# The last eight chunks of linear attention as pairs of 64 tokens, one step a slot

## The chip, the cores and the metric

The kernel runs on one core of one Trainium2 chip. The core has a matrix engine (TensorE, here PE, with its weight loads as PEld), a vector engine (DVE), a scalar engine (ACT) and a queue that issues DMAs (SP). The metric is the device time of one launch in microseconds (us); lower is better.

## The reference

```python
# linear attention with decay, 4 sequences x 8 heads x 768 tokens x 64
for t in range(S):
    state = gamma * state + einsum('bhd,bhe->bhde', k[:, :, t], v[:, :, t])
    y[:, :, t] = scale * einsum('bhd,bhde->bhe', q[:, :, t], state)
x = y as 3072 tokens x 512 features
# first MLP
h = x @ w_in                          # 512 -> 2048
x = (h * sigmoid(1.702 * h)) @ w_out  # 2048 -> 512
# second MLP, its own weights
h = x @ moe2_w_in
g = maximum(h, 0) + alpha * minimum(h, 0)
out = g @ moe2_w_out
```

All is float32; the kernel splits the operands of the MLPs into a high and a low part and multiplies those, and it runs attention in float32 itself.

## The kernel before

The 3072 tokens are 24 chunks of 128 (`C`), six to a sequence, and four chunks make a block of 512 columns (`BT`) for the MLPs. A state of 64x64 for each head is carried from chunk to chunk and starts anew every sixth chunk.

Attention runs beside the MLPs. A table `jobs` gives each piece of work a slot, and the MLP loops call `run(slot)` as they go. In the first part (slots up to 63, `base` = 64) a step of the first MLP on blocks 0 and 1 is 24 products of 512 columns and covers two slots. From then on (the loop over `units`, L1069) the MLPs run as seven products on a 2x2 grid of blocks; a unit is six products (`h_unit`, L763), and a slot comes after the fourth and after the seventh unit of each seven. Chunks 0 to 7 are done in the lead-in and the first part, chunks 8 to 15 in the first part from slot 36 on, and chunks 16 to 23 (the last eight) in slots `base` to `base` + 8, between the first units.

A chunk has two forms. In the **whole** form `att_scores` scales v on ACT (eight operations, L337), makes the scores of 128 tokens into two banks of PSUM (L344), and DVE multiplies both by the causal mask (L355). A slot later `att_out` (L372) makes the state update, the output from the chunk and the output from the state; `att_state` keeps the state in `diag` (L409, L412), and `att_x_kept` writes the outputs (L442). In the **half** form a chunk is two halves of 64 tokens, so that every product is 64x64 and uses a quarter of the array. `half_step(o, new)` issues in one step the outputs of the chunk before (`o`) and the scores and state updates of the next one (`new`), turn by turn (L481). DVE then masks the scores in one operation (L543), makes `mid`, the state between the halves (L557, or a copy on ACT at the start of a sequence, L555), the next state `hstate` (L561, L562), and the outputs (L572). `half_v_scale` (L471) scales v in a slot of its own, ahead of the step.

Before, chunks 8 to 15 are half and two slots apart, and all others whole. The two forms keep the state in another layout: `swap_state` moves it between them with three small DMAs on SP, once ahead of chunk 8 and once behind chunk 15.

q, k and v of the last eight come by `load_early(c)`, four DMAs of 256 KB on SP, in slots `LOADS` + `base`. Every engine takes its instructions in the order that the program's scheduler gave them, and `tc.high_priority` moves some ahead. That order is fixed when the program is built.

Of the kernel before, what the change touches and what calls it, by code (L numbers as in the profile page):

```python
# [19 lines left out]
P = 128  # L20
C = 128
# [54 lines left out]
def tile_linear_attention_two_mlps(ctx: ExitStack, tc, qk, kv, w1, w2, consts, alpha, out):  # L76
# [246 lines left out]
    att, xl = {}, {}  # L323

    def att_psum(c, which, shape):
        early = EARLY[c] if c < BT // C else EARLY[1] if c >= 4 * BT // C else {}
        if which in early:
            tag = early[which]
            return (ps_h if tag == "h" else ps_y).tile(shape, F32, tag=tag, name=which)
        return ps_a.tile(shape, F32, tag="a", name=which)  # L330
# [81 lines left out]
            nc.vector.tensor_tensor(out=diag, in0=src, in1=dec, op=ALU.mult)  # L412

    def att_x(c):
        if c >= 2 * BT // C:
            att_x_kept(c)
            return
        x32 = take("x32", (P, NP, C))
        early_x = c == BT // C - 1
        banks = att[c][0] if early_x else att[c]  # L420
        for n in range(2):
            px = banks[n][:, :2 * C].rearrange("p (n i) -> p n i", n=2)
            with tc.high_priority(HG):
                nc.vector.tensor_tensor(out=x32[:, n::2, :], in0=px, in1=decay_out[:, n::2, :], op=ALU.mult)
        j, i = divmod(c, BT // C)
        cols = slice(i * C, (i + 1) * C)
        if i == 0:
            new_x(j)
        nc.scalar.copy(out=x_hi[j][:, :, cols], in_=x32)  # L429
        if early_x:  # L430
            att_state(c)
        att[c] = x32

    def att_x_kept(c):
        banks = att.pop(c)
        t, i = divmod(c % (2 * BT // C), BT // C)
        for k in range(2):
            for d in range(2):
                if i == 0:
                    xl[k, d, t] = take("xl")  # L440
                with tc.high_priority(HG):
                    nc.vector.tensor_tensor(  # L442
                        out=xl[k, d, t][:, i * C:(i + 1) * C], in0=banks[k][:, d * C:(d + 1) * C],
                        in1=decay_out[:, 2 * d + k, :], op=ALU.mult,
                    )

    def att_x_low(c):
        j, i = divmod(c, BT // C)
# [12 lines left out]
        for s in range(2):  # L461
            nc.sync.dma_start(out=out[ROWS[s], 0::2, :], in_=src[ROWS[1 - s], 0::2, :])

    def half_psum(which):
        return (ps_h if which == "sc" else ps_a).tile([P, 512], F32, tag="h" if which == "sc" else "a", name=which)

    def half_v_scale(c):
# [59 lines left out]

    def half_step(o, new):
        if o is not None:
            att["px", o] = half_psum("px")  # L530
        if new is not None:
            att["sc", new] = half_psum("sc")
            att["pu", new] = half_psum("pu")
        half_products(o, new)
        if o is not None:
            give(att.pop(("v", o)), att.pop(("a", o)), att.pop(("mid", o)))
            leave("qk", o)
        if new is not None:
            leave("kv", new)
        with tc.high_priority(HG):  # L540
            if new is not None:
                a = att["a", new] = take("a", (P, 2 * NP, HC))
                nc.vector.tensor_tensor(  # L543
                    out=a, in0=att.pop(("sc", new)).rearrange("p (n i) -> p n i", i=HC),
                    in1=half_causal.unsqueeze(1).to_broadcast([P, 2 * NP, HC]), op=ALU.mult,
                )
                half_state(new)
            if o is not None:
                half_x(o)
# [13 lines left out]

    def half_x(c):
        px = att.pop(("px", c)).rearrange("p (n i) -> p n i", n=NP)
        n = c - 2 * BT // C
        t, i = divmod(n, BT // C)
        for k in range(2):
            for d in range(2):
                if i == 0:  # L570
# [332 lines left out]
    def job(slot, fn, *args, load=()):  # L903
        jobs.setdefault(int(slot), []).append((fn, args, load))

    def attention(c, s_scores, s_out, s_x, s_low):
        if c < 4 * per:
            job(s_scores, att_scores, c, load=(("qk", c), ("kv", c)))
        else:
            job(LOADS[c - 4 * per] + base, load_early, c)  # L910
            job(s_scores, att_scores, c)
        job(s_out, att_out, c)
        job(s_x, att_x, c)
        if c < 2 * per:
            job(s_low, att_x_low, c)

    def convert(key, slot):
        job(slot, conv_words, key, load=(key,))
# [8 lines left out]

    turn_at = {}
    for c in range(NCH):
        if 2 * per <= c < 4 * per:  # L930
            s = ATT1 + 2 * (c - 2 * per)
            turn_at.setdefault(s, {})["new"] = c
            turn_at.setdefault(s + 2, {})["o"] = c
            if c in RINGED:
                job(s - 1, half_v_scale, c, load=(("qk", c), ("kv", c)))
            else:
                job(s - 4, load_early, c)
                job(s - 1, half_v_scale, c)
            continue
        if c < per:  # L940
            s = 2 * c - 2 * per - 1
        elif c < 2 * per:
            s = 2 * (c - per)
        else:
            s = base + c - 4 * per
        attention(c, s, s + 1, s + 1, s + 2)
    for s, t in turn_at.items():
        job(s, half_step, t.get("o"), t.get("new"))
    job(2 * per + 4, swap_state, hstate[2 * per % 2], diag)
    job(ATT1 + 4 * per, swap_state, diag, hstate[4 * per % 2])  # L950
    for ft in range(NF):
        for n, kind in enumerate(("in", "out")):
            m = 2 * ft + n
# [218 lines left out]
```

## Time and profile before

| | |
|---|---|
| median of three timed runs | 1036.85 us (1035.78 to 1038.05) |
| profiled execution, span of its instructions | 1037.7 us |
| PE busy | 1019.7 us, 98% |
| DVE busy | 873.8 us, 84% |
| ACT busy | 679.3 us, 65% |
| DMA | 289.8 MB, 279 GB/s over the span |

The profiled execution is one run of its own; the page gives its span and nothing around it, and the span lies 0.85 us above the median. A busy PE is not PE at its peak: a product of 512 columns shows about 389 ns, but the next starts about 0.23 us after it, since they are pipelined. So what a stretch costs on PE is read from starts, not from busy time.

### The profile page before, as it was taken

The page shows a single profiled execution, that of the slowest core. Times are in us where ns is not written, and L with a number is a line of the kernel's source. Part 1 is how long each engine was busy: PE and PEld are TensorE (multiplying, and loading weights), DVE is VectorE, ACT ScalarE, POOL GpSimd, SP SyncE. Part 2 cuts the span into 40 slices and gives each one's busy share as a digit, 9 for nine tenths or more (in the row PEclk, how much of TensorE's full clock was granted, in tenths as well). Part 3 has the DMA queues.
Part 4 walks back from the last instruction along what each step waited for, and adds up shares of the span by engine and source line. Part 5 has one row for each costly group of instructions (what it writes and reads, how often), then busy time and mean ns, then how long its engine had stood idle before and what let it go on. Part 6 is the DMA issues. An engine that isn't in the chain of part 4 may idle for free.

```text
span 1037.7 us, 18658 instructions
## 1 busy us (share of the span) xinstructions
PE 1019.7 (98%) x6316; PEld 837.9 (81%) x6316; DVE 873.8 (84%) x1738; ACT 679.3 (65%) x1405; POOL 0.2 (0%) x4
## 2 busy tenths in 40 slices
PE   7999999898999999999999999999999999999998
PEld 5778888787888888888888888888888888888886
DVE  6999845997989999888899999998677978677792
ACT  6887835466776885765886776775555855556740
POOL 0000000000000000000000000000000000000000
PEclk9999999998999999999999999999999999999999
DMA  8689939689999889989989899896786766775671
GB/s 326 228 266 396 349 118 368 228 320 319 385 392 388 268 310 370 324 309 357 341 286 361 276 320 334 294 314 180 228 274 212 220 215 194 226 245 178 187 203 61
DMA packets 147231, 289.80 MB, mean 279 GB/s; under 512 B 17472, under 2 KB 17856, under 8 KB 147136
## 3 DMA queue, kind: packets, MB, share of 16 engines
q1 hardware_dynamic: 146848, 288.30, 80.8%
q8 instruction: 50, 0.82, 0.3%
q10 hardware_dynamic: 288, 0.31, 0.1%
q14 instruction: 45, 0.37, 0.1%
HBM read 213.83 MB, written 74.45 MB: 278 GB/s over the span
## 4 chain that ended last, share of the span: by engine, by line
PE 85%; DVE 8%; DMA 4%; ACT 1%; SPq 1%; issue 0%; DVEq 0%; ACTq 0%
PE py L836 37%; PE pa L763 21%; PE pd L763 16%; PE py L680 5%; PE ph L661 4%; DMA wcin<-wb 2%; DVE wb L229 1%; PE px L372 1%; DVE s L271 1%; PE sc L344 1%; DMA early<-kv 1%; DVE gl L645 1%; DMA ld<-kv 1%; DVE a L355 1%; DMA early<-qk 1%; DVE cvt L210 0%
## 5 line engine op out<-in xcount | busy, mean ns | idle before, releaser
L836 PE MATMUL py<-gh,yw 128*128 128x512 f32 x1120 | 299.5, 389 | 0.0
L836 PEld LDWEIGHTS py<-gh,yw 128*128 128x128 f32 x1120 | 210.2, 188 | 43.7
L763 PE MATMUL pa<-xo,hw 128*128 128x512 f32 x912 | 231.0, 390 | 0.0
L763 PEld LDWEIGHTS pa<-xo,hw 128*128 128x128 f32 x912 | 170.9, 188 | 35.8
L645 DVE TENSOR_TENSOR gl<-gw,gh 128x512 fp32r<-128x512 f32 x240 | 161.1, 687 | 42.9 <-ACT gh L644 36.9
L644 ACT CAST gh<-gw 128x512 fp32r<-128x512 f32 x240 | 145.7, 620 | 53.6 <-PE py L836 24.3
L763 PE MATMUL pd<-xo,hw 128*128 128x512 f32 x684 | 173.3, 389 | 0.0
L836 PE MATMUL py<-gl,yw 128*128 128x512 f32 x560 | 172.6, 389 | 0.0
L763 PEld LDWEIGHTS pd<-xo,hw 128*128 128x128 f32 x684 | 128.2, 188 | 26.8
L836 PEld LDWEIGHTS py<-gl,yw 128*128 128x128 f32 x560 | 105.1, 188 | 21.8
L850 DVE TENSOR_TENSOR yc<-py,yc 128x512 f32<-128x512 f32 x99 | 63.7, 684 | 26.2 <-PE py L836 26.2
L637 DVE SCALAR_TENSOR_TENSOR gw<-t,nalpha,gw 128x512 f32<-128x512 f32 x96 | 71.4, 748 | 15.5 <-ACT gw L636 15.3
L635 ACT ACTIVATE t<-gw 128x512 f32<-128x512 f32 x72 | 45.5, 632 | 52.7 <-DVE gw L778 49.8
L225 ACT CAST wb<-s 128x256 fp32r<-128x256 f32 x128 | 48.3, 402 | 41.4 <-DVE s L271 27.6
L680 PE MATMUL py<-gh,wb 128*128 128x512 f32 x256 | 67.3, 405 | 3.2 <-ACT gh L644 2.8
L661 PE MATMUL ph<-xhi,wb 128*128 128x512 f32 x256 | 64.2, 392 | 1.2 <-ACT xhi L429 1.2
L775 ACT COPY gw<-pa 128x512 f32<-128x512 f32 x80 | 46.8, 585 | 26.3 <-PE pa L763 25.7
L680 PEld LDWEIGHTS py<-gh,wb 128*128 128x128 f32 x256 | 47.9, 192 | 15.4 <-ACT gh L644 4.1
L661 PEld LDWEIGHTS ph<-xhi,wb 128*128 128x128 f32 x256 | 47.6, 188 | 11.6 <-ACT xhi L429 1.3
L778 DVE TENSOR_TENSOR gw<-pd,gw 128x512 f32<-128x512 f32 x80 | 54.8, 685 | 2.2 <-PE pd L763 2.1
L229 DVE TENSOR_TENSOR wb<-s,wb 128x256 fp32r<-128x256 f32 x128 | 50.0, 419 | 7.1 <-ACT wb L225 6.9
L799 DVE TENSOR_TENSOR gw<-gw 128x512 f32<-128x512 f32 x80 | 53.9, 688 | 0.3
(119 smaller groups left out, 1358.4 us busy)
## 6 DMA issues: line engine op xcount, KB each, us to landing
hw<-wcin SPq DMA_DIRECT2D x266, 256.0 KB, 4.7
yw<-wcout SPq DMA_DIRECT2D x232, 256.0 KB, 3.8
ld<-w SPq DMA_DIRECT2D x64, 512.0 KB, 5.9
wcin<-wb SPq DMA_DIRECT2D x112, 256.0 KB, 5.1
wcout<-wb SPq DMA_DIRECT2D x88, 256.0 KB, 4.2
yw<-wo SPq DMA_DIRECT2D x48, 256.0 KB, 5.1
wo<-wb SPq DMA_DIRECT2D x32, 256.0 KB, 6.3
early<-qk SPq DMA_DIRECT2D x26, 256.0 KB, 6.0
```

Of the source, the lines that this page charges most:

```text
L225: nc.scalar.copy(out=w[:, 0:256], in_=src)
L229: nc.vector.tensor_tensor(out=w[:, 256:], in0=src, in1=w[:, 0:256].bitcast(F32), op=ALU.subtract)
L637: nc.vector.scalar_tensor_tensor(out=g, in0=t, scalar=nalpha[:, ft:ft + 1], in1=g, op0=ALU.mult, op1=ALU.add)
L644: nc.scalar.copy(out=gh, in_=g)
L645: nc.vector.tensor_tensor(out=gl, in0=g, in1=gh.bitcast(F32), op=ALU.subtract)
L661: nc.tensor.matmul(out=ph, lhsT=cols(w, low, k), rhs=x[:, k, :], start=(n == 0), stop=(n == len(prods) - 1),)
L680: nc.tensor.matmul(out=py[e], lhsT=lhsT, rhs=g, start=(begin and seen[e] == 1), stop=(end and seen[e] == 3))
L763: nc.tensor.matmul(out=ps, lhsT=w[:, 256 * part_ + k * P:256 * part_ + (k + 1) * P], rhs=x[2 * k + low], start=(n in (0, 1, 3) and m == 0) ...
L778: nc.vector.tensor_tensor(out=g, in0=ps, in1=g, op=ALU.add)
L799: sub = lambda o, x, y: nc.vector.tensor_tensor(out=o, in0=x, in1=y, op=ALU.subtract)
L836: nc.tensor.matmul(out=ps[e], lhsT=w[:, at:at + P], rhs=t, start=(fresh and seen[e] == 1), stop=(m == GQ - 1 and seen[e] == 3), skip_group ...
L850: add_ = lambda o, x: nc.vector.tensor_tensor(out=o, in0=ps, in1=x, op=ALU.add)
```

## The change

Chunks 16 to 23 take the half form as well. Their steps come every slot (not every second one as for chunks 8 to 15), v is scaled one slot ahead of its step, and the loads keep their slots. Scores go to banks `y0` and `y3` in turn, state updates to `y1`, outputs to `y2`. The state stays in the half layout, so the second `swap_state` goes. The host lays out the arrays for all chunks from 8 on in halves.

```diff
     def att_x(c):
-        if c >= 2 * BT // C:
-            att_x_kept(c)
-            return
...
-    def half_psum(which):
+    def half_psum(which, c):
+        if c >= 4 * BT // C:
+            tag = {"sc": f"y{3 * (c % 2)}", "pu": "y1", "px": "y2"}[which]
+            return ps_y.tile([P, 512], F32, tag=tag, name=which)
         return (ps_h if which == "sc" else ps_a).tile([P, 512], F32, tag="h" if which == "sc" else "a", name=which)
...
     for c in range(NCH):
-        if 2 * per <= c < 4 * per:
-            s = ATT1 + 2 * (c - 2 * per)
+        if c >= 2 * per:
+            late = c - 4 * per
+            s, after = (base + late, 1) if late >= 0 else (ATT1 + 2 * (c - 2 * per), 2)
             turn_at.setdefault(s, {})["new"] = c
-            turn_at.setdefault(s + 2, {})["o"] = c
+            turn_at.setdefault(s + after, {})["o"] = c
             if c in RINGED:
                 job(s - 1, half_v_scale, c, load=(("qk", c), ("kv", c)))
             else:
-                job(s - 4, load_early, c)
+                job(LOADS[late] + base if late >= 0 else s - 4, load_early, c)
                 job(s - 1, half_v_scale, c)
             continue
-        if c < per:
-            s = 2 * c - 2 * per - 1
-        elif c < 2 * per:
-            s = 2 * (c - per)
-        else:
-            s = base + c - 4 * per
+        s = 2 * c - 2 * per - 1 if c < per else 2 * (c - per)
         attention(c, s, s + 1, s + 1, s + 2)
...
-    job(ATT1 + 4 * per, swap_state, diag, hstate[4 * per % 2])
```

What the change moves on the engines. On PE, the end of the first of the nine steps and the start of the second, with the units between (`sc` are scores, `pu` state updates and `px` outputs, each a bank of PSUM; `a` masked scores, `v` scaled v); before:

```order
L344 MATMUL sc_3503<-early 128x128
L763 MATMUL pa<-xo,wb 128x512 x12
L763 MATMUL pd<-xo,wb 128x512 x6
L372 MATMUL px<-v,early 64x64 x8
L372 MATMUL px<-a_3512,v 64x64
```

and now:

```order
L468 MATMUL sc<-early 64x64 x16
L468 MATMUL pu<-v,early 64x64 x16
L749 MATMUL pa<-xo,wb 128x512 x12
L749 MATMUL pd<-xo,wb 128x512 x6
L468 MATMUL px<-early,hstate_82 64x64
```

The steps stand at the same places between the units. The first step, which held eight rows of scores, now also holds the updates of the state, which stood in the second step before. Over all nine steps there were 296 rows and are 488; a row of a float32 product is two instructions in the trace. Elsewhere PE's order is the same.

On ACT, the end of the first part of the program, with the last two pairs of `g` and `gh`, the activations that the products `py` of the first MLP wait for (`v` is the scaled v, `wb` and `xo` are pieces of weights and of x); before:

```order
L632 ACTIVATE g_3270<-ph_3257 128x512
L644 CAST gh_3272<-g_3270 128x512
L225 CAST wb_3413<-s12_3356 128x256
L225 CAST wb_3421<-s34_3357 128x256
L225 CAST wb_3415<-s12_3356 128x256
L225 CAST wb_3423<-s34_3357 128x256
L588 CAST xo_3300<-xl_2577 128x512
L588 CAST xo_3300<-xl_2581 128x512
L632 ACTIVATE g_3338<-ph_3325 128x512
L588 CAST xo_3371<-t2_3121 128x512
L644 CAST gh_3340<-g_3338 128x512
```

and now:

```order
L458 ACTIVATE v_3539<-early_3320,cst_78 128x64 x5
L618 ACTIVATE g_3267<-ph_3254 128x512
L458 ACTIVATE v_3539<-early_3320,cst_78 128x64
L630 CAST gh_3269<-g_3267 128x512
L458 ACTIVATE v_3539<-early_3320,cst_78 128x64
L225 CAST wb_3419<-s12_3353 128x256
L225 CAST wb_3427<-s34_3354 128x256
L225 CAST wb_3421<-s12_3353 128x256
L574 CAST xo_3297<-xl_2577 128x512
L574 CAST xo_3297<-xl_2581 128x512
L618 ACTIVATE g_3335<-ph_3322 128x512
```

The scaling of v for chunk 17 (`v_3539`; one more of its eight stands just ahead of these rows) now comes ahead of the last two pairs of `g` and `gh`, and that of chunk 16 around the pair before those; both stood behind the last pair. Of the four casts of `wb` between the pairs three are left there, and the fourth comes behind the last `gh`.

On SP, the loads of chunk 17 (`early`, two for q and k and two for k and v), before:

```order
L249 DMA wcin1_6_96<-wb_3284 128x512
L249 DMA wcin1_6_96<-wb_3286 128x512
L286 DMA wo_3293<-wo0_122 128x512
L178 DMA early_3317<-qk 128x512
L178 DMA early_3319<-qk 128x512
L178 DMA early_3321<-kv 128x512
L178 DMA early_3323<-kv 128x512
```

and now:

```order
L178 DMA early_3218<-kv 128x512
L286 DMA wo_3294<-wo1_123 128x512
L178 DMA early_3314<-qk 128x512
L178 DMA early_3316<-qk 128x512
L178 DMA early_3318<-kv 128x512
L178 DMA early_3320<-kv 128x512
L249 DMA wcout1_7_113<-wb_3226 128x512
```

They stood behind the stores to `wcout1_7` and `wcin1_6` and now stand ahead of both.

## Rows read from the trace of the kernel before

**Rows 1.** The page, first part: busy time, share of the span, instructions.

```profile
PE 1019.7 (98%) x6316; PEld 837.9 (81%) x6316; DVE 873.8 (84%) x1738; ACT 679.3 (65%) x1405; POOL 0.2 (0%) x4
```

**Rows 2.** Windows: stretch, length, busy time by engine, clock, DMA share, GB/s.

```profile
246.00:320.00 74.00, 74.00 (x807) 60.61 (x806) 62.21 (x158) 49.33 (x124) 0.00 (x0) 0.99 1.01 373
```

**Rows 3.** Timeline of PE, whole steps: start, length, line, operation, tiles, shapes, count.

```profile
252.87 1.16 PE L344 MATMUL sc<-early 64*128 64x128 f32 x16
253.96 0.50 PE L763 MATMUL pa<-xo,wb 128*128 128x512 f32 x1
...
266.94 0.27 PE L372 MATMUL px<-a,v 128*64 128x64 f32 x1
...
269.47 1.66 PE L763 MATMUL pd<-xo,wb 128*128 128x512 f32 x6
...
282.01 0.69 PE L372 MATMUL px<-v,early 128*64 128x64 f32 x16
...
285.01 3.02 PE L763 MATMUL pa<-xo,hw 128*128 128x512 f32 x12
...
313.96 0.27 PE L372 MATMUL px<-a,v 128*64 128x64 f32 x1
315.40 0.73 PE L763 MATMUL pa<-xo,hw 128*128 128x512 f32 x2
```

**Rows 4.** Timeline of PE, half steps of chunks 8 to 15.

```profile
139.93 1.15 PE L481 MATMUL sc<-ld 64*64 64x64 f32 x32
...
141.94 2.11 PE L680 MATMUL py<-gh,wb 128*128 128x512 f32 x8
...
147.61 0.27 PE L481 MATMUL px<-ld,hstate 64*64 64x64 f32 x1
...
149.63 2.11 PE L680 MATMUL py<-gh,wb 128*128 128x512 f32 x8
...
206.52 0.68 PE L481 MATMUL px<-early,hstate 64*64 64x64 f32 x16
208.53 0.50 PE L680 MATMUL py<-gh,wb 128*128 128x512 f32 x1
```

**Rows 5.** Timeline of PE around 241 us; in brackets idle time and its releaser.

```profile
235.93 1.98 PE L680 MATMUL py<-gh,wb 128*128 128x512 f32 x8
...
241.65 3.78 PE L680 MATMUL py<-gh,wb 128*128 128x512 f32 x8 [2.84 <-ACT gh L644]
```

**Rows 6.** Windows, the stretch at the lower clock.

```profile
240.84:247.67 6.83, 6.02 (x14) 4.78 (x15) 5.56 (x12) 6.06 (x22) 0.00 (x0) 0.50 0.67 252
```

**Rows 7.** The chain of waits from 225 to 262 us: start, length, engine, tile, line.

```profile
236.83 1.09 DVE s L271 x3
...
238.63 0.03 ACT wb L225
...
241.07 0.53 ACT gh L644
```

**Rows 8.** Timeline of ACT.

```profile
233.61 0.62 ACT L644 CAST gh<-g 128x512 fp32r<-128x512 f32 x1
...
242.02 3.93 ACT L337 ACTIVATE v<-early,cst 128x64 f32<-128x64 f32 x16
```

**Rows 9.** Timeline of SP, DMA issues.

```profile
225.03 2.25 SPq L249 DMA_DIRECT2D wcout<-wb  x4
...
233.17 0.92 SPq L178 DMA_DIRECT2D early<-kv  x2
...
265.86 1.73 SPq L178 DMA_DIRECT2D early<-kv  x2
```

**Rows 10.** Tile `early` from 215 to 290 us.

```profile
DMA to landing us min/median/max: 3.8/5.3/6.3
```

**Rows 11.** Timeline of PE, a half step that waited.

```profile
196.64 0.29 PE L481 MATMUL px<-early,hstate 64*64 64x64 f32 x2 [1.66 <-DVE hstate L561]
...
200.86 0.50 PE L680 MATMUL py<-gh,wb 128*128 128x512 f32 x1
```

More of the change, by code (lines that the diff above doesn't have):

```diff
@@ L325, in att_psum @@
     def att_psum(c, which, shape):
-        early = EARLY[c] if c < BT // C else EARLY[1] if c >= 4 * BT // C else {}
+        early = EARLY[c] if c < BT // C else {}
         if which in early:
@@ L432, in att_x @@
         att[c] = x32
[L434 to L445, printed above, removed]
     def att_x_low(c):
@@ L529, in half_step @@
         if o is not None:
-            att["px", o] = half_psum("px")
+            att["px", o] = half_psum("px", o)
         if new is not None:
-            att["sc", new] = half_psum("sc")
-            att["pu", new] = half_psum("pu")
+            att["sc", new] = half_psum("sc", new)
+            att["pu", new] = half_psum("pu", new)
         half_products(o, new)
@@ L565, in half_x @@
         px = att.pop(("px", c)).rearrange("p (n i) -> p n i", n=NP)
-        n = c - 2 * BT // C
-        t, i = divmod(n, BT // C)
+        t, i = divmod(c % (2 * BT // C), BT // C)
         for k in range(2):
@@ L906, in attention @@
     def attention(c, s_scores, s_out, s_x, s_low):
-        if c < 4 * per:
-            job(s_scores, att_scores, c, load=(("qk", c), ("kv", c)))
-        else:
-            job(LOADS[c - 4 * per] + base, load_early, c)
-            job(s_scores, att_scores, c)
+        job(s_scores, att_scores, c, load=(("qk", c), ("kv", c)))
         job(s_out, att_out, c)
         job(s_x, att_x, c)
-        if c < 2 * per:
-            job(s_low, att_x_low, c)
+        job(s_low, att_x_low, c)
     def convert(key, slot):
@@ L936, in tile_linear_attention_two_mlps @@
             else:
-                job(s - 4, load_early, c)
+                job(LOADS[late] + base if late >= 0 else s - 4, load_early, c)
                 job(s - 1, half_v_scale, c)
             continue
-        if c < per:
-            s = 2 * c - 2 * per - 1
-        elif c < 2 * per:
-            s = 2 * (c - per)
-        else:
-            s = base + c - 4 * per
+        s = 2 * c - 2 * per - 1 if c < per else 2 * (c - per)
         attention(c, s, s + 1, s + 1, s + 2)
@@ L1140, in chosen @@
         n = np.arange(NCH)[:, None, None]
-        return np.where((n >= 2 * BT // C) & (n < 4 * BT // C), half, whole)
+        return np.where(n >= 2 * BT // C, half, whole)
     def weights(w_in, w_out, swap):
```

## The prediction

> **What bounds the kernel now.** I read the page first. PE is busy for 98% of the span, far ahead of DVE and ACT [rows 1]; since a busy PE need not be at its peak, that alone says only that PE seldom stands still. Next I cut out the stretch in which the last eight chunks run. From 246 to 320 us PE is busy for all of its 74.00 us, at a granted clock of 0.99 [rows 2]. So no wait is to be had there; time can only come from fewer or shorter products, and a stall of another engine costs something only if it becomes a wait of PE. The same row shows the DMA engines full (share 1.01, 373 GB/s). Third I read, from starts, what attention takes of PE there. Last I looked at the only long hole of PE near this stretch: it waits 2.84 us for `gh` ahead of 241.65 [rows 5], and from 240.84 to 247.67 the granted clock is 0.50, the lower of the two levels (1.2 of 2.4 GHz) [rows 6].
>
> **The steps on PE, before.** A step's price is the time from its first product to the next product of the units. The first (scores of chunk 16 alone) takes 253.96 - 252.87 = 1.09 us; a step at the edge of a sequence (outputs without state, or without an update) 269.47 - 266.94 = 2.53, and there are two; a full one 285.01 - 282.01 = 3.00, and there are five; the last (outputs alone) 315.40 - 313.96 = 1.44 [rows 3]. Sum: 1.09 + 2 x 2.53 + 5 x 3.00 + 1.44 = 22.59 us.
>
> **The steps after.** The trace of before has this very step, for chunks 8 to 15. With new work alone it takes 141.94 - 139.93 = 2.01 us for 64 instructions; with both parts 149.63 - 147.61 = 2.02 for 128; with old work alone 208.53 - 206.52 = 2.01 [rows 4]. The step with both takes no longer than one with half as much, because scores and outputs use different quarters of the array; that is where the gain is. Nine steps: 2.01 + 7 x 2.02 + 2.01 = 18.16 us. PE gains 22.59 - 18.16 = 4.43 us. The first step is dearer by 0.92 and the last by 0.57; the seven between give 5.9. The bounds: the steps could not well be under 2.0, so 4.6 at most; if products did not overlap, at the pace of the step with new work alone (2.01 / 64 = 31 ns), 976 instructions would take 30.6 us, a loss of 8.0. I take 4.43, because the same instructions in the same order were timed here.
>
> The Trainium skill speaks against the change on this point: "TensorE: Matmul & The Clock Gate", section "Wait — 56ns, not 53.3ns?", says that matmuls never start closer than about 25 ns, however few columns they have. By that, 976 instructions would take an estimated 24.4 us, and the change would lose 1.8. Here the trace disagrees: 2.02 us for 128 is 16 ns each [rows 4].
>
> **DVE and ACT.** For a chunk DVE does two masks, two state operations and four outputs before, and one mask, three state operations and the same four outputs after: one operation of 512 columns less, one of 256 more. ACT does one copy more for each sequence. PE never waits for either in this stretch [rows 2], so I count nothing for it. What counts is when they come, and three things move.
>
> First, the hole at 241.65. The chain of waits leads to it through DVE's sums (ending at 236.83 + 1.09 = 237.92), the last of four `wb` casts on ACT (238.63), and `gh` (ending 241.60) [rows 7]. In the new order that last cast stands behind `gh`. The third can start when the sums end, at about 238.0, so ACT gets to x and `g` some 0.6 us sooner, and PE starts at about 241.0. As PE then runs at half speed until 247.67 [rows 6], half of that is lost again: gain 0.3 us. Against it stands the scaling of v for chunks 16 and 17, now ahead of the last two pairs. Sixteen scalings took 3.93 us [rows 8], 0.25 each. Seven of chunk 17 come ahead of the next-to-last `gh`, which ended at 233.61 + 0.62 = 234.23 while PE wanted it at 235.93 [rows 5, 8]: 1.7 us more against a slack of 1.7, so a wait of 0.0 to 0.2. Those of chunk 16 stand around the pair before; ACT, idle for a third of the span [rows 1], should have room for them. Bounds for this place: 0.7 gained to 0.8 lost without a change of the clock; I take 0.2 gained.
>
> Second, the scaling now waits for a load. v of chunk 20 is scaled about a slot sooner than before, and its load is issued from 265.86 to 267.59 [rows 9] and lands about 5.3 us later [rows 10], so at up to 273. Behind half of that scaling stands the copy of `mid` for chunk 18 on ACT, behind that DVE's outputs of chunk 17, and for their bank the step of PE that I expect at about 273 (a slot of 7 to 8 us behind the one at 266.94 [rows 3], less 0.9 gained by then). If the load lands as late as before, this step waits 1 to 1.5 us. But four stores that stood ahead of the loads of chunk 19 go out earlier, while SP has little to do, so I expect the loads behind them some 2 to 3 us earlier. The copies of `pa` behind the scalings of chunks 21 and 22 have a slack of the same size. Bounds 0 to 2.5 us; I take 0.4 lost, near the lower end, because the order of the DMAs speaks for it.
>
> Third, the loads of the units' weights. PE reaches them up to 4.5 us sooner and DMA is full [rows 2]. The earlier stores help here too. I count nothing; at worst a wait of 1 us near 310.
>
> The three DMAs of the second swap go; nothing on PE waited for them.
>
> **Sum.** -4.43 - 0.2 + 0.4 = -4.2 us. Against the profiled execution that is a span of 1037.7 - 4.2 = 1033.5. The median of the runs lies 0.85 under that span, so the forecast is 1036.85 - 4.2 = 1032.6 us, 0.4% faster.
>
> **Rivals.**
>
> *The state comes late.* In chunks 8 to 15 one step waited for `hstate` on DVE, 1.66 us ahead of it, and then took 200.86 - 196.64 = 4.22 in place of 2.02 [rows 11]: 3.9 us in one step. DVE takes its work in a fixed order, and in the new one two of the state chains stand behind sums that wait for DMAs or behind the late copy of `mid`. Against it: the chain has a slot of some 8 us ((313.96 - 282.01) / 4 [rows 3]) and needs about 2 us of DVE, and the whole form, with the same slots and a chain of the same kind, made PE wait nowhere [rows 2]. One such wait gives 1032.6 + 3.9 = 1036.5, no change; a smaller one of 2 us gives 1034.6. Chance 0.17.
>
> *The clock stays up.* The hole at 241.65 gets shorter. If the clock does not fall there, PE is spared (247.67 - 241.65) / 2 = 3.0 us [rows 5, 6], and the time is 1029.6. For it: the fall came late in the hole, at 240.84, 0.8 us ahead of its end. Against it: the hole keeps more than 2 us. Chance 0.10.
>
> *The load of chunk 17 lands late (slower).* Seven scalings of it now stand on ACT ahead of a `gh` that PE wants at 235.93 [rows 5]. Before, that load was issued up to 234.1 [rows 9] and so landed at about 239 (5.3 us later, [rows 10]). If it still lands then, `gh` follows at about 242 (seven scalings 1.7, `g` and `gh` 1.2) and PE stands for 6 us; all that follows, the last hole too, moves by about 5.5, and the clock falls sooner or once more for up to 3.4 us. The sum is then between 1032.6 + 5.5 = 1038.1 and 1041.5; I put 1040. It decides from a landing at 237.8 on; up to 233 nothing is lost. Against it: the load now stands ahead of the stores that SP issued from 225.03 [rows 9], so it should land near 230. Chance 0.06.
>
> *The small products do not overlap*, in other banks than before, so that the change doesn't do what it says: 1032.6 + 4.4 + 8.0 = 1045 at the pace of 31 ns, or 1032.6 + 4.4 + 1.8 = 1038.8 by the 25 ns above. Against it: seven steps of the same form. Chance 0.03.
>
> **How the numbers follow.** The forecast has 0.64, and its own range is 1031 to 1034.4. What this kernel's measurement can tell from no change is about 0.2%, 2.1 us, so faster means under 1034.8. Faster: 0.64, and 0.10 for the clock, and about 0.03 of the late state with a small wait: 0.77. Same: the rest of the late state, 0.14, and 0.01 of the others. Slower: 0.08. The range for 8 in 10 goes from 1029.3, with the clock up, to 1035.3, with a wait of some 2.7 us.
>
> **What will show it.** Nine steps on PE of 2.0 us each, at the places of the old ones; PE busy throughout from about 246 to 316; the first `y` product behind the hole at about 241.0, and the clock at 0.50 behind it. The step after the start of the sequence at chunk 18 shows whether `mid` came late: any idle time of PE named for DVE or ACT there is the second item. The forecast is wrong if a step takes over 2.3 us, if PE waits anywhere from 246 to 316 for more than 1 us in sum, or if a hole appears at 236.

## The result, and the profile after

The change made the kernel slower. Its median is 1042.66 us over 6 runs (1040.14 to 1044.45), against 1036.48 us (1035.20 to 1038.05) of the kernel before in the same rounds; the ratio is 1.0054 [1.0041, 1.0067]. The forecast was 1032.6 us, with a range from 1029.3 to 1035.3.

The profiled executions show 3.6 us of this: the span is 1041.3 us, where it was 1037.7. In the kernel after and in every later run the span is 1.7 to 2.1 us shorter than the time of the same execution; by that, an estimate, the span of 1037.7 belongs to some 1039.5 us, more than any of the six runs of before here took, and so the spans show less of the loss than the medians. The page of the kernel after has these lines on the engines and on one DMA queue:

```profile
PE 1017.2 (98%) x6700; PEld 835.2 (80%) x6700; DVE 871.9 (84%) x1738; ACT 676.2 (65%) x1406; POOL 0.2 (0%) x4
...
q8 instruction: 54, 0.88, 0.3%
```

The first answers to [rows 1]. PE has 384 products more, and is busy for 2.5 us less, in a span that is longer: it stands still more. The last line is a queue that the prediction did not look at. It carries instructions, in packets of 16 KB, and will decide this case.

The stretch of [rows 2] is no longer full. By windows (busy time of PE, PEld, DVE, ACT, POOL, then granted clock, DMA share, GB/s):

```profile
243.00:317.00 74.00, 67.67 (x1161) 55.59 (x1161) 58.38 (x151) 44.99 (x114) 0.00 (x0) 0.95 0.97 356
...
283.53:286.95 3.42, 3.15 (x8) 2.50 (x9) 3.28 (x10) 2.50 (x10) 0.00 (x0) 0.50 1.02 382
293.77:297.19 3.42, 3.42 (x9) 2.71 (x9) 1.88 (x7) 0.56 (x1) 0.00 (x0) 0.50 1.04 385
```

PE is idle for 6.3 of 74 us, and the granted clock is at its lower level twice, for 3.42 us each, where it was there once, from 240.84 to 247.67 [rows 6]. PE's own rows, from its timeline (in brackets idle time and its releaser), show where it stands:

```profile
240.53 0.73 PE L666 MATMUL py<-gh,wb 128*128 128x512 f32 x2 [2.00 <-ACT gh L630]
243.39 0.84 PE L749 MATMUL pa<-xo,wb 128*128 128x512 f32 x3
...
272.04 0.50 PE L749 MATMUL pa<-xo,hw 128*128 128x512 f32 x1 [0.36 <-ACT gw L618]
...
278.69 0.21 PE L468 MATMUL px<-early,hstate 64*64 64x64 f32 x1 [0.91 <-DVE s L271]
...
283.80 0.76 PE L749 MATMUL pa<-xo,hw 128*128 128x512 f32 x1 [3.02 <-ACT gw L618]
...
293.20 0.21 PE L468 MATMUL pu<-v,early 64*64 64x64 f32 x1 [1.80 <-issue]
...
317.40 0.97 PE L749 MATMUL pa<-xo,hw 128*128 128x512 f32 x3
```

The first row answers to [rows 5]: that hole went from 2.84 to 2.00 us and the clock did not fall in it, so the units start at 243.39, 3.55 us ahead of before. What follows gives more than that back. The nine half steps, from their first product to the next product of the units, as [rows 3] were read:

```
start   248.92 255.24 262.93 269.26 278.69 289.57 300.99 307.69 315.38
length    2.01   2.02   2.02   2.78   5.12   4.13   2.38   2.04   2.01   sum 24.5 (forecast 18.16)
```

Five are what was forecast. The fourth, fifth, sixth and seventh are not, and 0.91 us of waiting stands ahead of the fifth. From the first unit to the product behind the last step PE took 315.40 - 246.94 = 68.46 us before and takes 74.01 now, 5.55 more; the start 3.55 sooner leaves 2.0 us lost on PE. The other 1.6 us of the profile lie behind PE's last product (5.92 us to the end of the span, 4.32 before), in the landing of the last outputs; later runs show 4.3 there for kernels like before and anything from 4.2 to 6.3 for kernels like after, so I leave it out.

### The profile page after: what moved, and what is told of

Same layout as the page of the kernel before. It is cut to its first block, busy times and chain, and to the rows that moved or that the text cites. A ratio compares the mean times of both kernels' runs of the same rounds, so it can differ in the third digit from the quotient of the medians.

```text
span 1041.3 us, 19427 instructions
## 1 busy us (share of the span) xinstructions
PE 1017.2 (98%) x6700; PEld 835.2 (80%) x6700; DVE 871.9 (84%) x1738; ACT 676.2 (65%) x1406; POOL 0.2 (0%) x4
## 4 chain that ended last, share of the span: by engine, by line
PE 77%; DVE 10%; DMA 7%; ACT 4%; issue 1%; SPq 0%; DVEq 0%; ACTq 0%
PE py L822 37%; PE pa L749 20%; PE pd L749 15%; DMA ld<-kv 3%; PE ph L647 2%; DVE wb L229 2%; PE py L666 2%; DMA early<-kv 1%; DVE s L271 1%; DMA ld<-w 1%; DMA wcin<-wb 1%; DVE gl L631 1%; PE px L468 1%; ACT v L458 1%; DVE cvt L210 1%
```

## The experiments

Four theories stood at one time or another. A: ACT stands for late loads at the head of its queue (it does wait: four times, 8.1 us in all), and what is queued behind it holds PE. B: PE runs out of instructions. C, later D: DVE is late for the next step; as D, it frees the one PSUM bank of `px` too late. F: what PE gains is given back to engines that are full.

Two numbers are counted in each trace. PE's instructions (weight loads, products, semaphore instructions) are numbered by their start, from 0: 13,766 after, 12,993 before. Divided by 256 that is 53.8 and 50.8, and the queue q8 carries 54 packets of 16 KB after and 50 before, so one packet is 256 instructions of 64 bytes. The page of before:

```profile
q8 instruction: 50, 0.82, 0.3%
```

And the holes at 283.80 and 293.20 stand at the numbers 6081 and 6337, the wait at 278.69 at 5825: each leaves 193 when divided by 256. Such a number is called a border. The fifth half step (5825 to 6080) is exactly one packet. Count the packets along with the borders, the first packet for 449, the next for 705, and so on: PE passes none of the 1043 borders of the 20 traces sooner than 2.18 us behind the start of its packet.

Each trace is one execution, and executions of one program differ. PE's 2000th product of the program's own, which comes ahead of the place of every edit but e3's, starts between 191.67 us (e13) and 196.01 (e6); e14 and e18 are the same program, and are 2.7 us apart at the 2200th (206.10 and 208.79). So times are compared by medians and intervals, and the traces are read for where PE stands.

**First four: theory A against theory B.** e1 moves the loads, e2 the scaling of v, e3 the packets' borders, e4 does to the kernel before what A blames.

```diff
-LOADS = (-5, -3, -1, 1, 2, 3, 4, 5)                                       # e1
+LOADS = (-6, -4, -2, -1, 0, 1, 2, 3)
-                job(s - 1, half_v_scale, c)                               # e2, chunks 16 to 23, ranked ahead of half_step
+                job(s, half_v_now, c)
+    for _ in range(64):                                                   # e3, behind the warm products
+        nc.tensor.matmul(out=idle[:, :32], lhsT=warm[:, :P], rhs=warm[:, :32], start=True, stop=True)
+            job(s_scores - 1, whole_v_scale, c)                           # e4, in the kernel before
```

> The changed kernel with the loads of the last eight chunks one to two slots earlier (slots -6, -4, -2, -1, 0, 1, 2, 3 from the start of the late part, where they were -5, -3, -1, 1, 2, 3, 4, 5); nothing else differs. Theory A (ACT: the scaling of v now stands one slot nearer to its load, waits for it at the head of ACT's queue, and the gates and copies behind it hold PE): the wait of 2.91 us ahead of 276.64 and the PE hole of 3.02 us ahead of 283.80 go, and with the hole one of the two stretches at the lower clock (3.41 us, half of it lost, 1.7): 1042.7 - 4.7 = 1038. Theory B (PE runs out of instructions inside dense half steps): the hole of 1.80 us inside a half step stays or moves to another one; by B alone the time stays within 1 us of 1042.7. Theory C (DVE's chain of state and products of x is late): no hole of PE ahead of a half step goes, 1042 to 1043.

> The changed kernel with v of chunks 16 to 23 scaled in the slot of its half step, ahead of it, and not one slot before; loads as in the changed kernel. Theory A: ACT's waits for loads (8.1 us in four waits) shrink to under 1 us, since each load has some 7 us more; but the update products of the same half step now wait for eight scalings of 0.25 us, so up to 2 us of PE in each of eight steps: between 1038 (the scalings find ACT free) and 1050. Theory B: the hole of 1.8 us inside one half step stays, whatever ACT does; alone 1042.7. Theory C: no change, 1042 to 1043.

> The changed kernel with 64 more products of 32 columns on PE at the very start, beside the warm products, where PE waits for the first loads: 128 instructions, half of one 16 KB packet of instructions (64 bytes each, by 0.88 MB in 54 packets and one packet per 256 instructions). Theory B: where the packets begin within the late half steps moves by half a packet, so the hole of 1.80 us inside the half step at 289.57 goes and one like it comes in another half step, or none: 1039 to 1043. Theory A and theory C: the hole at 293.20 has nothing to do with packets and stays where it is; 1042.7.

> The kernel before, its last eight chunks in their whole form, with one difference: v of chunks 16 to 23 is scaled one slot earlier, as in the changed kernel, with the loads where they were. Theory A: ACT stands for the loads as in the changed kernel, and gates and copies behind it hold PE: one hole of about 3 us and one stretch at the lower clock of 1.7 us lost, 1036.5 + 3 to 5 = 1039.5 to 1041.5. Theory B and theory C: nothing that they speak of is changed, 1036.5 within 1 us.

Measured: e1 1044.63 us, ratio to before 1.0073 [1.0056, 1.0090]; e2 1040.47, 1.0033 [1.0019, 1.0047]; e3 1040.73, 1.0041 [1.0026, 1.0057]; e4 1037.51, 1.0004 [0.9993, 1.0015].

As the cause of the two large holes theory A falls with e1. ACT waits for no load there any more, and both are there, at the same instruction numbers 6081 and 6337. PE's timeline of e1, and ACT's gate that the first row names:

```profile
285.52 0.63 ACT L618 ACTIVATE gw<-gw 128x512 f32<-128x512 f32 x1 [0.34 <-DVE gw L764]
```

```profile
286.70 4.46 PE L749 MATMUL pa<-xo,hw 128*128 128x512 f32 x12 [2.90 <-ACT gw L618]
...
297.08 0.27 PE L468 MATMUL px<-early,mid 64*64 64x64 f32 x1 [2.74 <-issue]
```

The gate had ended 0.55 us before PE went on, so it did not hold PE; a releaser is inferred, and here it is only the last thing that happened. In the kernel after it ended at 283.79, by chance just ahead of 283.80. e2 shows the same hole without such a chance:

```profile
277.77 0.21 PE L471 MATMUL px<-early,hstate 64*64 64x64 f32 x1 [0.20 <-DVE s L271]
...
283.43 4.56 PE L752 MATMUL pa<-xo,hw 128*128 128x512 f32 x12 [3.57 <-issue]
```

e3 moves the borders by half a packet, and all nine half steps take 2.01 to 2.02 us; one wait of 1.95 us for `px` is left, ahead of a step. Its time is little better, though: 1.0041, with an interval that overlaps that of the kernel after (1.0041 to 1.0067). Its trace is 3.7 us behind the one of the kernel after at PE's 2000th product, and its own products take 1.75 us there; what made the rest is not shown, and e6, whose edit comes later, is 2.9 behind at the same product. e4 says little on A, as its ACT waits for a load only 0.40 us.

**Next four: moving the borders in an idle place.** The same small products stand where PE waits for `gh` at 240.

```diff
+    fill = ps_a.tile([P, 512], F32, tag="a", name="fill")
+    some = cst.bitcast(BF16)
+    for _ in range(54):                                                   # e5, e7, e8; 80 in e6
+        nc.tensor.matmul(out=fill[:, :32], lhsT=some[:, :P], rhs=some[:, :32], start=True, stop=True)
     for s, step in queue:
         finish_step(s, step)
```

> The changed kernel with 54 small products of 32 columns (108 PE instructions) put where PE waits for gh before the last step ahead of the units, 2.00 us there; at the 27 ns apiece that 64 like them took at the start of e3 (1.75 us) they need 1.5 us, inside that wait. Theory B (instructions): PE's instructions come in packets of 256, and all three late holes (0.91, 3.02, 1.80 us) stand at instruction numbers that leave 193 when divided by 256, since from 5825 to 6081 a whole packet is one half step, used up in 2.0 us. 108 instructions more move the borders so that no packet is used up in under 5.4 us by the steps' own times: the three holes (5.7 us) go, and with them the two stretches at the lower clock (3.41 us each, half of it lost, 3.4 together): 1042.7 - 9.1 = 1033.6. Theory A (ACT waits for loads): nothing of it is changed, the waits of ACT for loads (8 us) stay, and the hole of 3.02 us charged to the gate stays: 1042.7 or at best 1041 for the clock ahead.

> As e5, but 80 products (160 instructions, 2.2 us of work in the same wait). Theory B: the borders now lie so that the seventh half step, the one that starts at 300.99 in the changed kernel, is a whole packet of its own (2.0 us): the holes at the fourth to sixth half step go, and one of 2 to 3 us comes at the end of the seventh, with a stretch at the lower clock (1.7 us): 1033.6 + 0.2 + 4 = 1038, and some 4 us slower than e5. Theory A: 54 and 80 products make no difference, and no hole comes at the seventh half step.

> The kernel before with the same 54 products in the same place, its late chunks whole. By theory B no packet there is used up in under 9 us in that part, so moving the borders does nothing; what is left is what filling the wait does to the clock: 3.41 to 6.83 us at the lower clock in the kernel before, of which half is lost: 1036.9 - 0 to 3.4 = 1033.5 to 1036.9. If e5 gains far more than this one, the filler's effect on e5 is that of the borders.

> e5 and the earlier loads of e1 together, so that neither ACT's waits nor the packets should be left. Theory B: within 1 us of e5. Theory A, in so far as ACT's waits for loads cost time beside the packets: 1 to 3 us under e5. Earlier loads that hurt by themselves (e1 measured 1044.6): 1 to 3 us above e5.

Measured: e5 1038.87 us, 1.0019 [1.0004, 1.0033]; e6 1044.65, 1.0065 [1.0048, 1.0082]; e7 1037.54, 1.0000 [0.9986, 1.0014]; e8 1042.24, 1.0044 [1.0031, 1.0057].

80 products against 54 make 5.8 us; at 27 ns apiece the 26 more explain 0.7 of it. How much of the rest is the place of a border is not shown: the stretch of the half steps is 71.15 us in the trace of e6 and 69.61 in that of e5, and e6 is 3.5 us behind already at the 2000th product, ahead of the edit. The hole came where theory B had it, at the seventh half step and behind (PE, e6), now at the numbers 6849 and 7105:

```profile
301.69 1.55 PE L749 MATMUL pd<-xo,hw 128*128 128x512 f32 x6 [1.11 <-ACT cvt L192]
...
310.75 0.33 PE L468 MATMUL px<-early,mid 64*64 64x64 f32 x4 [2.87 <-issue]
```

But e5 kept only 3.8 of the 9.1 us that B promised. With the border holes gone, other waits stand in their place (PE, e5): `px` held by DVE, and far behind, a gate with a stretch of 3.41 us at the lower clock. This trace is of the longest of e5's 11 executions, 3.4 us above their median, so not all of it need stand in the others.

```profile
286.72 0.24 PE L468 MATMUL px<-early,hstate 64*64 64x64 f32 x1 [1.91 <-DVE xl L558]
...
412.74 1.65 PE L749 MATMUL pa<-xo,hw 128*128 128x512 f32 x6 [2.31 <-ACT gw L618]
```

e8 has the first kind too (3.00 us ahead of 289.39), and the earlier loads again gained nothing.

**The bank of px.** The late half steps stand one slot apart, and their `px` has one bank, `y2`; DVE reads it in four scalings that stand among its other work.

```diff
-            tag = {"sc": f"y{3 * (c % 2)}", "pu": "y1", "px": "y2"}[which]
+            tag = {"sc": "y0", "pu": "y1", "px": f"y{2 + c % 2}"}[which]   # e9; e10 with e5's, e11 = e2 + e5, e12 = e2 + e5 + e9
```

> The changed kernel with two PSUM banks in turn for px of the late half steps and one for the scores, where it has one for px and two for the scores. Theory D (one bank of px: a half step's px products wait until DVE has scaled the px of the step before, one slot earlier): seen in e5 as 3.1 us of PE in three waits, but in the changed kernel only as far as the packet borders leave it. Theory B: the holes at PE instructions 6081 and 6337 (3.02 and 1.80 us) stay, since no instruction of PE is added: 1041 to 1043. Theory D alone: 1042.7 - 3 = 1039.7.

> The two banks for px together with the 54 products of e5. Theory D: e5 (1038.9) less its 3.1 us of px waiting for DVE: 1035.8. If those waits are DVE being late anyhow, the next step waits for the state instead (hstate, mid) and it stays at 1038 to 1039.

> e2 (v scaled in the slot of its half step) with the 54 products of e5. In e2 the only late hole over 0.25 us is 3.57 us at PE instruction 6081, a packet border, with one stretch of 3.41 us at the lower clock behind it. Theory B with theory A: the border hole goes, and with it the stretch: 1040.5 - 3.6 - 1.7 = 1035.2, under the kernel before. Theory D: px waits for DVE as in e5, 3 us: 1038 to 1039.

> All three: v scaled in the step's slot, two banks for px, 54 products ahead of the units. If packets (B), ACT's order (A) and the bank of px (D) are all that stood against the change, the late half steps cost 9 x 2.02 and nothing waits: the forecast of 4.2 us under the kernel before plus what the filled wait gives, 1032 to 1035. If another wait takes their place, 1036 to 1039.

Measured: e9 1035.71 us, 0.9994 [0.9981, 1.0007]; e10 1040.16, 1.0029 [1.0014, 1.0045]; e11 1040.00, 1.0025 [1.0009, 1.0042]; e12 1039.87, 1.0025 [1.0012, 1.0039].

I had it the wrong way round: two banks alone, without a border moved, take some 7 us away (1042.66 to 1035.71, and the intervals are far apart), and the combinations do not add up. In e9 the border 6081 stands where it stood, and costs 0.25 us. The same product of PE, the gate on ACT that stood charged with its wait, and the stretch by windows:

```profile
281.81 3.04 PE L749 MATMUL pa<-xo,hw 128*128 128x512 f32 x12 [0.25 <-ACT cvr L194]
```

```profile
282.90 0.63 ACT L618 ACTIVATE gw<-gw 128x512 f32<-128x512 f32 x1 [0.64 <-DVE gw L764]
```

```profile
246.00:311.00 65.00, 64.51 (x1170) 53.06 (x1169) 53.90 (x141) 42.91 (x108) 0.00 (x0) 1.00 1.02 378
```

PE goes on 1.7 us before that gate ends. What changed is the packet: it started at 279.55, 0.08 us behind the head of the step (279.47); in the kernel after it started at 281.20, 2.51 behind the head (278.69). From 281.1 to 282.2 us of the kernel after and from 279.4 to 280.6 us of e9 the queue has one packet each (packets, MB, share of 16 engines):

```profile
q8 instruction: 1, 0.02, 5.4%
```

```profile
q8 instruction: 1, 0.02, 5.0%
```

**Last six: is it the border, the bank, or both; and what is left.** e13 is e6 with two banks, e14 (and e18, the same again) is e2 with two banks, e15 and e16 spread the second layer's conversions, e17 keeps one bank and frees it sooner.

```diff
-W2_AT = [3 + 1.17 * m for m in range(12)] + ...
+W2_AT = [5 + 1.5 * m for m in range(12)] + ...                             # e15 (with e9's edit), e16 (before)
+        first = o is not None and o >= 4 * BT // C                         # e17
         with tc.high_priority(HG):
+            if first:
+                half_x(o)
...
-            if o is not None:
+            if o is not None and not first:
                 half_x(o)
```

> e6 with two banks for px: as in e6, the seventh half step is one whole packet of PE's instructions (borders at 6849 and 7105), where e6 had holes of 1.12 and 2.87 us. Theory BD (both are needed: only where the head of such a step waits for the px bank is the next packet asked for too late): no wait ahead of the seventh half step and no hole over 0.5 us at 7105; time some 4 to 6 us under e6's 1044.7, so 1039 to 1041. Theory B (borders alone): the hole of some 2.9 us at 7105 stays, and the time within 2 us of e6.

> e9 (two banks for px) with v scaled in the slot of its half step, as in e2; borders as in the changed kernel. Theory BD: in e2 the one late hole was 3.57 us at 6081, behind a step whose head waited 0.20 us for px; with two banks both go, 1040.5 - 3.6 - 1.7 = 1035.2, as e9. Theory A: ACT's waits for loads cost e9 some more, and this kernel is 1 to 2 us under e9's 1035.7.

> e9 with the first twelve conversions of the second layer's weights started later and further apart (from 5 + 1.5 m slots behind the start of the late part, where they stood at 3 + 1.17 m): each loads 512 KB and stores its pieces, and the late half steps run while the DMA engines are full (share 1.03 to 1.05 from 260 to 300 us). Theory F (DMA: what PE gains there is given back waiting for loads and stores): with less traffic in the stretch PE keeps more of the gain: 1 to 3 us under e9's 1035.7, and the kernel before with the same edit (e16) gains less, since its PE never waits there. Theory BD: nothing, within 1 us of e9, unless the conversions come to lack room later.

> The kernel before with the same edit as e15, as its control. Theory F: within 1 us of 1037.2, as PE does not wait in this stretch. If it gains or loses as much as e15, the edit's effect has nothing to do with the half steps.

> The changed kernel with one edit: in the late half steps DVE scales px of the old chunk together and ahead of the state of the new one, where the four scalings stood between the state's operations; banks, borders and ACT's order as in the changed kernel. px is free some 0.5 to 1 us sooner after each step. Theory BD: if with that the fifth half step, which began 0.42 us behind the last scaling, does not wait, the holes of 3.02 us at instruction 6081 and 1.80 us at 6337 shrink to under 0.5 us, and the time comes to 1036 to 1038, near e9; if it still waits a tenth, the hole of 3 us stays whole. If instead the number of banks for the scores mattered: 1042.7, with the holes there and no wait at the head.

> e14 once more, timed in other rounds. e14 gave 0.9989 [0.9974, 1.0004] of the kernel before; if it is really faster, again 0.998 to 0.9995.

Measured: e13 1038.21 us, 1.0004 [0.9986, 1.0022]; e14 1036.12, 0.9989 [0.9974, 1.0004]; e15 1042.79, 1.0046 [1.0029, 1.0063]; e16 1043.66, 1.0058 [1.0039, 1.0076]; e17 1039.33, 1.0014 [1.0001, 1.0026]; e18 1036.55, 0.9994 [0.9979, 1.0008].

e13 against e6 is 6.4 us, with the same borders, and the intervals are apart: the hole of 2.87 us at 7105 is gone. In the two traces the stretch is 3.1 us shorter (68.09 for 71.15); the rest lies ahead of the units, and is not shown to come from the bank. The hole at 6849 stays (PE, e13), so a border alone can cost a microsecond:

```profile
295.52 1.44 PE L749 MATMUL pd<-xo,hw 128*128 128x512 f32 x5 [0.95 <-issue]
```

e14 and e18 against e2 is the third pair that differs by the bank alone, and again the intervals are apart. e18 has 1.10 us at 6081 where e14, the same program, has under 0.25: that part differs from one execution to the next. e17 broke the theory as I had written it. The fifth step did not wait at all, and the hole behind it was the longest of all (PE, e17):

```profile
282.67 0.70 PE L752 MATMUL pa<-xo,hw 128*128 128x512 f32 x2 [3.83 <-ACT gw L621]
```

What orders all of these is not PE's wait but the time at which DVE freed `px`. DVE's last scaling ahead of the fifth step, in the kernel after, ends at 277.79 + 0.48 = 278.27:

```profile
277.79 0.48 DVE L558 TENSOR_TENSOR xl<-px,cst 128x128 f32<-128x128 f32 x2
```

Read in the same way, for the packet that each of these steps runs into (us; head is the step's first product):

```
kernel, step        px free   head     packet starts   packet behind px free   hole
after, fifth         278.27   278.69       281.20             2.93              3.02
after, sixth         287.69   289.57       290.73             3.04              1.80
e1, fifth            281.27   281.42       284.24             2.97              2.90
e1, sixth            290.83   292.50       294.62             3.79              2.74
e2, fifth            277.38   277.77       280.88             3.50              3.57
e6, eighth           304.50   305.90       308.34             3.84              2.87
e17, fifth           276.30   276.75       280.22             3.92              3.83
e2, sixth            285.41   289.29       287.81             2.40              none
e17, sixth           284.73   288.56       287.23             2.50              none
e9, fifth (2 banks)    -      279.47       279.55               -               0.25
e14, fifth (2 banks)   -      278.36       278.15               -               none
e18, fifth (2 banks)   -      278.44       279.27               -               1.10
```

In the nine rows with one bank the packet starts 2.4 to 3.9 us behind the moment when `px` is free, however long the step has been due; and PE's first instruction behind the border starts 2.3 to 2.5 us behind the packet's start in all rows but the two sixth steps without a hole, which come to the border later than that. Where `px` is free 3.8 us ahead of the step, nothing shows. So the holes of 1.8 to 3.8 us need both: a border inside the step or at its end, and `px` freed late; a border alone costs up to 1.1 us (e13, e18).

Both together are not yet enough. The sixth steps of e3, e5 and e6 waited 1.95, 1.91 and 1.96 us for `px`, a border fell 0.4 to 0.8 us behind their heads, and each took 2.02 us all the same: a late `px` cost its own wait and no more. Their packets had started 2.5 to 4.4 us before `px` was free. What differs is the border before: it lies 168, 149 and 200 instructions ahead of the step's first `px` product there, and at most 41 ahead in the nine rows (in e1's fifth step one behind). The time is not fixed, though: in the last steps of e5, e8 and e11, with a border 2 to 9 instructions ahead, the packet started 1.2 to 1.5 us behind `px` free. That it is PE's sequencer which stands at the first `px` product, and asks for the next packet only behind it, is inferred from this order; no record shows the request. The Trainium skill ("Advanced Engine Details and Errata", section "Sequencer and Instruction Queues") has the sequencer read the next instruction and push it into a queue for the engine, and the instruction wait for its semaphores; a read-ahead that such a wait can stop fits the table, and no run here shows how long the queue is. One rival is left: each run with two banks for `px` also has one bank for the scores, where the kernel after has two, and no run changes one of these alone. Against it stands e17, which keeps two for the scores and frees `px` sooner: the hole at its sixth step is gone.

e15 and e16 settle nothing. Both lost 3.16 us ahead of 518 us and more behind, the control as much as the other, and the stretch of the half steps took 65.48 us in e15 against 64.84 in e9.

## Why the prediction was wrong

The stretch from the first unit to the product behind the last half step, and PE's time from there to its last product, worked out from starts in each trace:

```
kernel                first unit   stretch   from there on    median us, this | before in the same rounds
before                  246.94      68.46       717.98         1036.48
e4 (before, v early)    245.48      68.20       717.98         1037.51 | 1037.26
e7 (before, filled)     243.25      68.81       719.56         1037.54 | 1037.21
after                   243.39      74.01       717.99         1042.66 | 1036.48
e17 (px free sooner)    243.00      69.33       717.99         1039.33 | 1037.14
e5 (54 products)        242.32      69.61       724.37         1038.87 | 1037.21
e9 (two banks)          245.89      64.84       719.57         1035.71 | 1037.25
e14 (e9, v in step)     244.75      64.77       718.36         1036.12 | 1038.24
e18 (e14 again)         244.18      69.93       718.03         1036.55 | 1037.14
```

*The step that failed* is the first, "The steps after": "I take 4.43, because the same instructions in the same order were timed here". The products were priced rightly, and the place they stand in was not. Five steps took 2.01 to 2.04 as forecast. But the steps of chunks 8 to 15 come every 7.7 us (139.93, 147.61 [rows 4]), the late ones every 6.3 and 7.7 in turn (255.24, 262.93, 269.26), with one bank for `px` that DVE has to free in between; and 256 instructions in 2.0 us are a whole packet, where a whole step of before had 160 in 3.0. The working put DVE at nothing here, since PE waits for it nowhere in [rows 2], and the supply of instructions did not stand in it at all. The sum for the stretch was 68.46 - 4.43 + 0.4 = 64.4; it took 74.0. Of the 9.6 us between, 6.1 are the four holes (0.36 + 0.91 + 3.02 + 1.80), 0.4 each a halt inside the fourth step (2.78 - 0.36 - 2.02) and the longer seventh (2.38 - 2.02), and 2.9 the two stretches at the lower clock (half of the 3.15 and 3.42 us that PE worked in them, less the 0.37 that before lost behind 246.94): 9.8 in sum. In e9 and e14, at 64.8, 3.6 of the 4.43 came, so it can be had on PE. It is not had in every execution: e18, the program of e14 once more, took 69.93, with waits of 0.61, 1.10 and 1.79 us and a stretch at the lower clock; e14's trace is of the shortest of its 12 executions.

*The trace of before had the warning.* In the half steps of chunks 8 to 15, PE has a hole with no releaser inside a step:

```profile
200.59 0.21 PE L481 MATMUL pu<-v,early 64*64 64x64 f32 x1 [1.85 <-issue]
```

It stands at instruction 4289, a border (193 again), in the very step that [rows 11] was quoted for; I read those 4.22 us as the price of a late state.

*First, the hole at 241.65*: it became 0.84 us shorter, near the 0.6 of the working. But the clock did not fall there, so the units began 3.55 us sooner, as in the rival "The clock stays up". How much of that the change made is not shown. e16, the kernel before with an edit that comes later, starts its units at 245.00, with 3.41 us at the lower clock where the trace of before has 6.83; and of e14 and e18, one program, the clock fell there in the first (3.41 us from 241.37) and not in the second. Here it was lost again, and more: PE was idle 3.02 and 1.80 us later on, and each time the clock went to its lower level for 3.4 us.

*Second, the scaling that waits for a load*: right that it waits, and more than I thought (8.1 us of ACT, with 2.91 ahead of 276.64). It cost PE what the working put down, 0.4, and on the path it named. The scaling of chunk 20 waited 0.67 us for its load, `mid` was copied behind half of it until 269.25, DVE freed the bank of `px` at 269.91, and the fourth step, begun at 269.26, could start its `px` products at 270.05, 0.79 behind its head; in e1, where no scaling waits, that is 0.29. By the chain of waits the 0.36 behind that step hangs on the same load. Beyond that no run shows a cost: e1 took all these waits away and was no faster (1.0073 [1.0056, 1.0090]). I would have named it as the cause of the large holes from the profile alone, since the gate and the load stand in the chain of waits.

*Third, the loads of the units' weights* and the swap: no wait of PE for them. *The state comes late*: PE waited 0.91 us for DVE, but for the bank of `px`, not for the state. *The load of chunk 17* and *the small products do not overlap*: neither.

*Would the forecast have come true without the holes?* Not quite. e9 and e14 take 3.6 us off the stretch in their traces, and e9, e14 and e18 still are level with the kernel before (0.9994, 0.9989 and 0.9994, each interval holding 1). Part is given back behind it: 1.6 us in e9, 0.4 in e14. e7 shows this without any half step: its filled wait lets the units start 2.2 us sooner than in e4, and at PE's last product both are equal (1031.63 and 1031.66). There a gate waits at 678:

```profile
678.10 1.66 PE L763 MATMUL pa<-xo,hw 128*128 128x512 f32 x6 [1.20 <-ACT gw L636]
```

In e10, where PE was as early, ACT stood 5.84 us for a store to leave its tile, while the DMA engines were full (share 1.03 from 280 to 300 us), and PE 1.92 us behind it:

```profile
301.43 0.62 ACT L630 CAST gh<-gw 128x512 fp32r<-128x512 f32 x1 [5.84 <-DMA wcin<-wb]
```

So a PE that is busy throughout [rows 2] did not mean that all it gains is kept. Why e10 to e12 are 4.2 to 4.5 us slower than e9 can be read in part from this store. By the traces ACT stands for its landing 5.84, 7.19 and 4.81 us in e10 to e12 and 5.01 in e18, and PE right behind it, for a gate at the eighth step, 1.92, 3.46, 2.27 and 1.79 us, each time with a stretch of 3.41 us at the lower clock; in e9 and e14 ACT stands 2.47 and 2.63, and PE not at all, and the kernels before and after have no such wait. The length of ACT's wait alone does not decide it: in e13 it is 5.47, and PE stands 0.37. No run takes this wait away, so that it is the whole difference is not shown, nor that theory F holds for all of what is missing.

## What to carry to other kernels

When many small instructions replace few large ones, count instructions per microsecond as well as time per product, and look for a wait with no releaser in the stretch that already works so. When steps move closer together, count the banks of each tile that passes from one step to the next: one bank freed just in time looks free in the trace, and here the next packet of instructions came 2.4 to 3.9 us behind it. A releaser in a profile is a guess: move the thing it names, and see whether the hole goes.

## What the hardware showed that I had not expected

PE's instructions come over the same DMA engines as the data, during the run: 54 packets of 16 KB, 0.9 to 1.1 us each in this stretch where the DMA share is 0.97, and PE goes on 2.3 to 2.5 us behind the start of the packet that it waits for. A half step of 2.02 us uses up one packet of 256 instructions. Where the borders between packets fall counts: a hole of 2.87 us stood at 7105 in e6, and with two banks at the same border it was gone (e13).
